# Opening of a Fourier-mixing and GEGLU stack: x loaded one transfer ahead, six rows of tiles in float32, and five S1 tiles summed by transfers

## The chip, the core and the metric

The kernel runs on one core of one Trainium2 chip. The metric is the device time of one execution in microseconds (us); the time before is 1612.5 us, the median of three runs (1612.4 to 1614.12). The engines named below are TensorE (PE, with its weight loads PEld), VectorE (DVE), ScalarE (ACT), GpSimd (POOL) and SyncE (SP). A transfer (DMA) is issued from the instruction stream of SP or of POOL, and an engine executes its own stream in order.

## The reference

```python
def _A_ref(x, dft_seq_re, dft_seq_im, dft_hid_re, dft_hid_im):
    a = jnp.einsum("bsd,ed->bse", x, dft_hid_re)
    b = jnp.einsum("bsd,ed->bse", x, dft_hid_im)
    return jnp.einsum("ts,bse->bte", dft_seq_re, a) - jnp.einsum("ts,bse->bte", dft_seq_im, b)

def _B_ref(x, w_gate, w_up, w_down):
    return (_gelu(x @ w_gate) * (x @ w_up)) @ w_down

x = A_x                                   # (1, 2048, 512) float32
x = x + _A_ref(_layernorm(x), ...)        # layer 0
x = x + _B_ref(_layernorm(x), ...)        # layer 1, hidden size 1792
x = x + _A_ref(_layernorm(x), ...)        # layer 2
x = x + _B_ref(_layernorm(x), ...)        # layer 3
```

## The kernel before

**Arithmetic.** A float32 operand is split into a high part (`hi`, ScalarE, line 147) and a remainder (`lo`, VectorE, line 149), both of type fp32r, and a product of two split operands is three matmuls (`mm3`, lines 196 to 198). The sequence transform of layer 0 and layer 2 is done in four blocks of 512 output rows (`b` = 0 to 3). Real and imaginary parts and the two halves of the sequence make a two by two block product, which is done with seven products in the manner of Strassen and Winograd. Their names are A11, A12, S2, S1, S3, S4 and A22 on the side of the transform (`ws`, 128x512 tiles from memory) and B11, B21, T2, T1, T3, T4 and B22 on the side of the normed rows. Each product runs over `k` = 0 to 7, that is over eight tiles of 128 rows. S1 is A21 + A22, S2 is S1 - A11, S3 is A11 - A21 and S4 is A12 - S2.

**Order of layer 0.** `plan` puts A11 of all four blocks first, then A12 of all four, and then, block by block, S2 (with S1 and S3 two and four steps behind, `skewed(3)`), products with the hidden transform, and S4. For A11 of block 0 alone (`bare`, line 409) nothing is split: `a11` (line 755) multiplies the normed tile `za[k]` and the loaded tile in plain float32 (line 761). Every other product goes through `six` (line 738), which takes two times three matmuls for each `k`. The sums of A12 with A11 for blocks 1 to 3 are added on VectorE (line 184) and put away to memory by POOL (`put_away`, line 251, tensors `m` and `m_sum`). The tiles that they leave are used again as slots.

**Slots and streams.** All 128x512 tiles live in 94 slots (`Slots`, line 98). `items` is the list of what TensorE will take, in order, with the tiles each needs and how it is made; `load_next` (line 285) issues the loads of an item from SP, four items ahead of the splitting, and `split_next` makes it. `make_s2` (line 349) does three VectorE operations on 128x512 tiles: `plus(a22, a21, a22)` (line 187) gives S1, and two `minus` (line 180) give S3 and S2; the split of S2 follows. A load into a slot waits for the last reader of what was in it, and each of the two streams of transfers has eight semaphores in turn, so that a transfer also waits for the one eight places before it.

**The opening.** A row tile of x is loaded (`x_load`, line 224) and normed (`norm_terms`, line 499): VectorE takes the statistics (lines 507 and 509), POOL raises to the power -0.5 (line 515), VectorE makes the shift (line 519), and from the fifth tile on POOL does what VectorE did after line 509 (lines 512 and 517). ScalarE then writes the normed tile (lines 548 and 550), and `first_parts` splits half of it (256 columns, lines 147 and 149). The loads alternate: x 0, ws 0, x 1, ws 1 and so on to x 7 and ws 7 (line 1357). Twelve matmuls on a constant tile (line 1347) come first on TensorE. Steps of the queue `queue` (`opening`, `second_opening`, `combine`, `combine_late`) are run between the products, and put the rest of the norming and the sums T1 to T4 into the streams. The scheduler orders the instructions of each engine from this program when the kernel is built.

**The last layers.** In layer 3 the down products of the first half of the rows are taken from pieces stored in memory (`wc`), and the weights of the second half's first gate and up products (`wb`) are fetched in that stage: `ahead` (line 1282) is a list of eight `piece_load` steps, put at the head of the queue one third of the way through (line 1316), ahead of the steps that bring in and divide the rows of the second half.

Of the kernel before, what the change touches and what calls it, by code (L numbers as in the profile page):

```python
# [14 lines left out]
P = 128  # L15
# [28 lines left out]
def fnet_geglu(ctx: ExitStack, tc: tile.TileContext, x_in, ws, wh, wgu, wdn, wdc, out):  # L44
# [113 lines left out]
    def split_slot(src):  # L158
        hi, lo = sb.get(F32R), sb.get(F32R)
        split(src, hi, lo)  # L160
        return hi, lo
# [20 lines left out]
    def plus(out, a, b):  # L182
        if id(b) in ps8.held:
            bank_read["DVE"] = nc.vector.tensor_tensor(out, a, b, op=ALU.add)  # L184
        else:
            with behind("DVE"):
                nc.vector.tensor_tensor(out, a, b, op=ALU.add)  # L187
# [97 lines left out]
    def load_next():  # L285
        n = stream["loaded"]
        dtype, addresses, _, _ = items[n]
        raws[n] = []
        for a in addresses:
            t = sb.get(dtype)  # L290
            to = t if dtype == F32 else f32(t)
            if len(a.shape) == 3:
                to = to.rearrange("p (h c) -> p h c", h=2)
            stream["last"] = nc.sync.dma_start(to, a)
            raws[n].append(t)
        stream["loaded"] += 1

    def too_far(n):
# [43 lines left out]
    def make_a11(k):  # L342

        def run(v):
            held[k] = v
            return split_slot(v)
        return run

    def make_s2(k):
        def run(a21, a22, *a11):  # L350
            a11 = a11[0] if a11 else held.pop(k)
            plus(a22, a21, a22)
            minus(a21, a11, a21)
            minus(a11, a22, a11)
            s1s[k], s2s[k], s3s[k] = a22, a11, a21
            return split_slot(a11)
        return run

    def make_s1(k):
# [46 lines left out]
            steps += products  # L406
        return steps

    def bare(layer, b, what):

        return layer == 0 and b == 0 and what == "A11"


    NP = NF // 2
# [15 lines left out]
    def mix_items(layer):  # L430
        def raw(make, *tiles):
            items.append((F32, tiles, make, None))

        for b, what in plan(layer):
            tiles = [[ws[(b * 2 + m) * NS + k] for k in range(NS)] for m in range(2)]
            (a11, a12), (a21, a22) = ((r[:NK], r[NK:]) for r in tiles)
            hold = b >= FORE[layer]
            if what == "A11":
                for k in range(NK):
                    raw(as_is if bare(layer, b, what) else make_a11(k) if hold else plain, a11[k])  # L440
            elif what == "A12":
                for k in range(NK):
                    raw(plain, a12[k])
            elif what == "S2":
                for i, k in skewed(3):
                    if i == 0:
                        raw(make_s2(k), a21[k], a22[k], *(() if hold else (a11[k],)))
                    else:
                        raw(make_s1(k) if i == 1 else make_s3(k))
            elif what == "S4":  # L450
                for i, k in skewed(2):
                    if i == 0:
                        raw(make_s4(k), a12[k])
                    else:
                        raw(plain, a22[k])
            else:
                for m, c in what:
                    if layer == 0 and b == 0:
                        items.append((F32, (wh[m * ND + c],), make_hid_first(m, c), (m, c)))
                    else:  # L460
                        items.append((F32R, halves(whs[m, c]), make_hid(m, c), (m, c)))
# [26 lines left out]
            slow.pop(0)()  # L488


    known, shifts = {}, []

    def row_of(layer, i, mixed):
        x = fresh.pop(("mixed", i) if mixed else i, None)
# [4 lines left out]
    def norm_terms(layer, i, x, junk):  # L499

        pool = spool if layer == 0 else kpool
        rstd = pool.tile([P, 1], F32, name="rstd")
        shift = pool.tile([P, 1], F32, name="shift")
        if layer == 0 or layer == 2 and i >= NS - NK:
            st = spool.tile([P, 6], F32, name="st")
            with tc.issue_after(shifts[-1].ins) if layer == 0 and i == 1 else ExitStack():
                nc.vector.bn_stats(st, x)
            mv = spool.tile([P, 2], F32, name="mv")
            nc.vector.bn_aggr(mv, st)
            late = layer == 0 and i >= 4  # L510
            if late:
                nc.gpsimd.tensor_scalar(rstd, mv[:, 1:2], 1.0, EPS, op0=ALU.mult, op1=ALU.add)  # L512
            else:
                nc.vector.tensor_scalar_add(rstd, mv[:, 1:2], EPS)
            nc.gpsimd.tensor_tensor(rstd, rstd, power, op=ALU.pow)
            if late:
                nc.gpsimd.tensor_scalar(shift, mv[:, 0:1], -1.0, rstd, op0=ALU.mult, op1=ALU.mult)
            else:
                shifts.append(nc.vector.scalar_tensor_tensor(shift, mv[:, 0:1], -1.0, rstd, op0=ALU.mult, op1=ALU.mult))  # L519
        else:  # L520

            total = spool.tile([P, 1], F32, name="total")
            mean = spool.tile([P, 1], F32, name="mean")
            nc.scalar.activation(junk, x, AF.Copy, accum_out=total)  # L524
            nc.scalar.activation(mean, total, AF.Copy, scale=-1.0 / D)
            nc.scalar.activation(junk, x, AF.Square, bias=mean, accum_out=rstd)  # L526
            nc.gpsimd.tensor_scalar(rstd, rstd, 1.0 / D, EPS, op0=ALU.mult, op1=ALU.add)  # L527
            nc.gpsimd.tensor_tensor(rstd, rstd, power, op=ALU.pow)
            nc.scalar.activation(shift, mean, AF.Copy, scale=rstd)
        return rstd, shift  # L530
# [30 lines left out]
    def first_parts(k):  # L561
        zparts["11", k] = split_side(za[k][:, half[0]])
# [134 lines left out]
    def mix(layer):  # L697
# [57 lines left out]
        def a11(b):  # L755
            chain = [ps8.get() for _ in range(2)]
            for k in range(NK):
                if bare(layer, b, "A11"):
                    t, = take()
                    for c in range(2):  # L760
                        nc.tensor.matmul(chain[c], za[k][:, c * P:(c + 1) * P], t, start=k == 0, stop=k == NK - 1)
                    sb.put(t)
                    step()
                else:
                    six(chain, "B11", k, k == 0, k == NK - 1, "11" if b == NB - 1 else None)
            sums[b] = [copied(p) for p in chain]
            if b < FORE[layer]:
                ps8.put(*chain)
            else:
                chains[b] = chain  # L770
# [178 lines left out]
    def geglu(w, layer):  # L949
# [333 lines left out]
        if plain_down:  # L1283
            for f in range(NF - LAG, NF):
                down(f, 0)
            add_rows(0)
            if before_mix:
                for k in range(NT):
                    queue.extend([lambda k=k: second_rows(layer + 1, k), lambda k=k: combine(k)])
                queue.extend([lambda k=k: combine_late(k) for k in range(NT)])  # L1290
            else:
                queue.extend(ahead)
            for f in range(NF):
                if f == NF - 2:
                    load_rows(1)
                down(f, 1)
                while len(queue) > 2 * (NF - 1 - f):
                    step()
            add_rows(1, before_mix)
        else:  # L1300
            if pairs == NP:
                pair_combined(NP - 1)
            late = down_order(layer, w)[1]
            for i, (name, k) in enumerate(late):
                for more in late[i:i + EARLY + 1]:
                    prepared(*more)
                for _ in down_product(name, k):
                    pass
                if not before_mix or i % 3 == 0:
                    step()  # L1310
                if before_mix and i == len(late) // 2:
                    stream["more"] = MORE
                if i == len(late) // 3:
                    load_turned(1)
                    if w == 0:
                        queue[:0] = ahead
                while w == 0 and len(queue) > 2 * (len(late) - 1 - i):
                    step()
            if pairs < NP:
                plain_rows()  # L1320
# [31 lines left out]
    def x_ahead(i):  # L1352
        if i < NS and i not in loaded:
            loaded.add(i)
            fresh[i] = x_load(0, i)

    for i in range(NK):
        x_ahead(i)
        load_next()

    def opening(k):

        def run():
            x_ahead(k + 2)
            if k < NK:
                first_norm(0, k)
            first_parts(k - 2)
        return run

    def second_opening(k):  # L1370
# [64 lines left out]
```

## Time and profile before

| what | us |
|---|---|
| median of three runs | 1612.5 |
| the profiled execution, its own time | 1614.3 |
| the profiled execution, span from first to last instruction | 1612.5 |
| PE busy | 1604.7 |
| DVE busy | 1171.6 |
| ACT busy | 816.9 |
| POOL busy | 275.2 |

The profile gives busy times by engine, the idle time ahead of groups of instructions with what ended it, the chain of work that ended last, and a timeline. Starts are counted from the start of the span. A matmul is shown with a busy time longer than the distance to the next one, since matmuls are pipelined; the distance between their starts is what counts. A float32 matmul that is not split shows as two records.

### The profile page before, as it was taken

The page shows a single profiled execution, that of the slowest core. Times are in us where ns is not written, and L with a number is a line of the kernel's source. Part 1 is how long each engine was busy: PE and PEld are TensorE (multiplying, and loading weights), DVE is VectorE, ACT ScalarE, POOL GpSimd, SP SyncE. Part 2 cuts the span into 40 slices and gives each one's busy share as a digit, 9 for nine tenths or more (in the row PEclk, how much of TensorE's full clock was granted, in tenths as well). Part 3 has the DMA queues.
Part 4 walks back from the last instruction along what each step waited for, and adds up shares of the span by engine and source line. Part 5 has one row for each costly group of instructions (what it writes and reads, how often), then busy time and mean ns, then how long its engine had stood idle before and what let it go on. Part 6 is the DMA issues. An engine that isn't in the chain of part 4 may idle for free.

```text
span 1612.5 us, 22750 instructions
## 1 busy us (share of the span) xinstructions
PE 1604.7 (100%) x7046; PEld 1322.2 (82%) x7046; DVE 1171.6 (73%) x2023; ACT 816.9 (51%) x1564; POOL 275.2 (17%) x497
## 2 busy tenths in 40 slices
PE   9999999999999999999999999999999999999999
PEld 6888888888888888888888888888888888888887
DVE  7997878789876665666889978877874557844574
ACT  7753453545766434555757433644445535433360
POOL 3211010142544113220031000110410000000001
PEclk9999999999999999999999999999999999999999
DMA  9767787899978799986895776968989777796455
GB/s 360 240 233 261 263 273 240 267 320 318 349 275 301 226 353 305 378 298 230 290 304 177 251 250 205 315 206 310 273 284 277 236 227 218 242 301 193 147 180 157
DMA packets 250090, 424.67 MB, mean 263 GB/s; under 512 B 28848, under 2 KB 90032, under 8 KB 248944
## 3 DMA queue, kind: packets, MB, share of 16 engines
q1 hardware_dynamic: 223488, 334.33, 65.2%
q0 software_dynamic: 26480, 88.89, 15.0%
q8 instruction: 56, 0.92, 0.2%
q14 instruction: 66, 0.54, 0.1%
HBM read 339.48 MB, written 83.62 MB: 262 GB/s over the span
## 4 chain that ended last, share of the span: by engine, by line
PE 91%; DMA 4%; DVE 2%; issue 1%; POOL 1%; ACT 0%; SPq 0%; DVEq 0%; ACTq 0%; POOLq 0%
PE p L196 30%; PE p L198 30%; PE p L197 30%; DMA s<-ws 2%; DVE s L149 1%; DVE s L180 1%; DMA s<-x 0%; DMA s<-wc 0%; POOL rstd L512 0%; ACT s L147 0%; DMA s<-wb 0%; DMA xwide<-ws 0%; DMA m_sum<-s 0%; DVE s L184 0%; DMA xwide<-t 0%
## 5 line engine op out<-in xcount | busy, mean ns | idle before, releaser
L197 PE MATMUL p<-s,s 128*128 128x512 f32 x2330 | 904.6, 389 | 0.0
L198 PE MATMUL p<-s,s 128*128 128x512 f32 x2330 | 896.1, 389 | 0.0
L196 PE MATMUL p<-s,s 128*128 128x512 f32 x2330 | 864.9, 390 | 1.3 <-DMA s<-wb 0.7
L147 ACT ACTIVATE s<-s 128x512 fp32r<-128x512 f32 (+1 forms) x785 | 445.1, 606 | 327.7 <-PE p L197 66.0
L149 DVE TENSOR_TENSOR s<-s,s 128x512 fp32r<-128x512 f32 (+1 forms) x785 | 492.1, 660 | 92.7 <-ACT s L147 76.9
L196 PEld LDWEIGHTS p<-s,s 128*128 128x128 f32 x2330 | 437.1, 188 | 94.3 <-ACT s L147 2.2
L197 PEld LDWEIGHTS p<-s,s 128*128 128x128 f32 x2330 | 437.3, 188 | 91.2 <-DVE s L149 0.3
L198 PEld LDWEIGHTS p<-s,s 128*128 128x128 f32 x2330 | 437.3, 188 | 90.8
L184 DVE TENSOR_TENSOR s<-s,p 128x512 f32<-128x512 f32 x286 | 192.5, 682 | 211.7 <-PE p L198 120.3
L191 ACT ACTIVATE s<-p 128x512 f32<-128x512 f32 x218 | 127.6, 592 | 133.1 <-PE p L198 121.3
L180 DVE TENSOR_TENSOR s<-s,s 128x512 f32<-128x512 f32 (+1 forms) x323 | 192.5, 612 | 2.0 <-DMA s<-ws 0.7
L946 ACT ACTIVATE s<-s 128x512 f32<-128x512 f32 x103 | 64.7, 629 | 87.3 <-DVE s L184 85.5
L147 ACT ACTIVATE s<-xwide 128x512 fp32r<-128x512 f32 x83 | 50.8, 622 | 65.7 <-PE p L197 14.0
L527 POOL TENSOR_SCALAR rstd<-rstd 128x1 f32<-128x1 f32 x40 | 20.7, 518 | 341.4 <-ACT s L526 335.0
L149 DVE TENSOR_TENSOR s<-xwide,s 128x512 fp32r<-128x512 f32 x83 | 56.0, 681 | 23.6 <-ACT s L147 23.2
L278 POOL DMA_DIRECT2D wb<-s x84 | 45.4, 543 | 58.3 <-ACT s L147 45.8
L550 ACT ACTIVATE s<-s,shift,rstd 128x512 f32<-128x512 f32 x56 | 45.0, 810 | 19.7 <-DVE shift L519 9.4
L524 ACT ACTIVATE s<-s 128x512 f32<-128x512 f32 x33 | 20.8, 630 | 64.2 <-PE p L198 34.1
L960 DVE TENSOR_TENSOR s<-s,s 128x512 f32<-128x512 f32 x75 | 51.7, 689 | 1.8
L240 POOL DMA_DIRECT2D x<-s x31 | 17.0, 549 | 141.1 <-DVE s L184 134.4
L187 DVE TENSOR_TENSOR s<-s,s 128x512 f32<-128x512 f32 (+1 forms) x67 | 39.5, 607 | 0.6 <-DMA s<-wgu 0.6
L184 DVE TENSOR_TENSOR xwide<-s,p 128x512 f32<-128x512 f32 x13 | 8.9, 687 | 41.5 <-PE p L198 41.5
(97 smaller groups left out, 567.8 us busy)
## 6 DMA issues: line engine op xcount, KB each, us to landing
s<-ws SPq DMA_DIRECT2D x384, 256.0 KB, 4.5
s<-wb SPq DMA_DIRECT2D x294, 256.0 KB, 5.1
s<-wc SPq DMA_DIRECT2D x133, 256.0 KB, 4.4
s<-wh SPq DMA_DIRECT2D x116, 256.0 KB, 5.1
wb<-s POOLq DMA_DIRECT2D x98, 256.0 KB, 4.4
s<-x SPq DMA_DIRECT2D x63, 256.0 KB, 5.4
xwide<-ws SPq DMA_DIRECT2D x52, 256.0 KB, 5.0
wc<-s POOLq DMA_DIRECT2D x49, 256.0 KB, 6.0
```

The source lines that it names most:

```text
L147: newest["ACT"] = nc.scalar.activation(hi, src, AF.Copy)
L149: newest["DVE"] = nc.vector.tensor_tensor(lo, src, f32(hi), op=ALU.subtract)
L180: nc.vector.tensor_tensor(out, a, b, op=ALU.subtract)
L184: bank_read["DVE"] = nc.vector.tensor_tensor(out, a, b, op=ALU.add)
L191: bank_read["ACT"] = nc.scalar.activation(v, src, AF.Copy)
L196: nc.tensor.matmul(ps, ah, bh, start=start, stop=False, skip_group_check=True)
L197: nc.tensor.matmul(ps, ah, bl, start=False, stop=False, skip_group_check=True)
L198: nc.tensor.matmul(ps, al, bh, start=False, stop=stop, skip_group_check=True)
L278: nc.gpsimd.dma_start(a, f32(t))
L550: nc.scalar.activation(z, x, AF.Identity, bias=shift, scale=rstd)
L946: nc.scalar.activation(t, g, AF.Gelu_apprx_tanh)
L960: nc.vector.tensor_tensor(t, t, v, op=ALU.mult)
```

## The change

Five edits are made together.

- The first loads are x 0, then x 1, ws 0, x 2, ws 1 and so on: x is one transfer ahead of ws, and x 8 is loaded ahead of ws 7.
- A11 of block 0 is done in plain float32 for `k` = 0 to 5 alone. For `k` = 6 and 7 it goes through `six`, in the same accumulation, so that two more ws tiles are split, and the splits of the normed tiles 6 and 7 are made earlier (`opening`).
- On VectorE the statistics of a row tile of layer 0 are issued after the small operations of the tiles one and two before it.
- For block 0 of layer 0 and `k` = 3 to 7, S1 is not added on VectorE. After the load of an item, POOL issues a transfer that reads A21 from memory a second time and adds it to the A22 tile on chip.
- In layer 3 the eight `piece_load` steps are put into the queue in turn with the steps already there, and no longer all ahead of them.

```diff
@@ load_next
             stream["last"] = nc.sync.dma_start(to, a)
             raws[n].append(t)
+        if getattr(items[n][2], "summed", False):
+            nc.gpsimd.dma_start(raws[n][1], addresses[0], accum_op=ALU.add)
@@ make_s2
-    def make_s2(k):
+    def make_s2(k, summed):
         def run(a21, a22, *a11):
             a11 = a11[0] if a11 else held.pop(k)
-            plus(a22, a21, a22)
+            if not summed:
+                plus(a22, a21, a22)
             minus(a21, a11, a21)
             minus(a11, a22, a11)
...
+        run.summed = summed
@@ bare, mix_items
-    def bare(layer, b, what):
-        return layer == 0 and b == 0 and what == "A11"
+    def bare(layer, b, what, k):
+        return layer == 0 and b == 0 and what == "A11" and k < 6
...
-                        raw(make_s2(k), a21[k], a22[k], *(() if hold else (a11[k],)))
+                        raw(make_s2(k, layer == 0 and b == 0 and k >= 3), a21[k], a22[k], *(() if hold else (a11[k],)))
@@ norm_terms
-            with tc.issue_after(shifts[-1].ins) if layer == 0 and i == 1 else ExitStack():
+            late = layer == 0 and i >= 4
+            with ExitStack() as order:
+                if layer == 0:
+                    for at in (("rstd", i - 1), ("shift", i - 2)):
+                        if at in first_small:
+                            order.enter_context(tc.issue_after(first_small[at].ins))
                 nc.vector.bn_stats(st, x)
@@ a11
-                        nc.tensor.matmul(chain[c], za[k][:, c * P:(c + 1) * P], t, start=k == 0, stop=k == NK - 1)
+                        nc.tensor.matmul(chain[c], za[k][:, c * P:(c + 1) * P], t, start=k == 0, stop=False, skip_group_check=True)
@@ geglu
-                        queue[:0] = ahead
+                        queue[:2 * len(ahead)] = [run for pair in zip(ahead, queue) for run in pair] + queue[len(ahead):2 * len(ahead)]
@@ the opening
+    x_ahead(0)
     for i in range(NK):
-        x_ahead(i)
+        x_ahead(i + 1)
         load_next()
...
-            first_parts(k - 2)
+            for j in (k - 2,) if k < 7 else (5, 6) if k == 7 else (k - 1,) if k <= NK else ():
+                first_parts(j)
```

More of the change, by code (lines that the diff above doesn't have):

```diff
@@ L439, in mix_items @@
                 for k in range(NK):
-                    raw(as_is if bare(layer, b, what) else make_a11(k) if hold else plain, a11[k])
+                    raw(as_is if bare(layer, b, what, k) else make_a11(k) if hold else plain, a11[k])
             elif what == "A12":
@@ L488, in step @@
             slow.pop(0)()
-    known, shifts = {}, []
+    known, first_small = {}, {}
     def row_of(layer, i, mixed):
@@ L509, in norm_terms @@
             nc.vector.bn_aggr(mv, st)
-            late = layer == 0 and i >= 4
             if late:
@@ L513, in norm_terms @@
             else:
-                nc.vector.tensor_scalar_add(rstd, mv[:, 1:2], EPS)
+                first_small["rstd", i] = nc.vector.tensor_scalar_add(rstd, mv[:, 1:2], EPS)
             nc.gpsimd.tensor_tensor(rstd, rstd, power, op=ALU.pow)
@@ L518, in norm_terms @@
             else:
-                shifts.append(nc.vector.scalar_tensor_tensor(shift, mv[:, 0:1], -1.0, rstd, op0=ALU.mult, op1=ALU.mult))
+                first_small["shift", i] = nc.vector.scalar_tensor_tensor(
+                    shift, mv[:, 0:1], -1.0, rstd, op0=ALU.mult, op1=ALU.mult
+                )
         else:
@@ L757, in a11 @@
             for k in range(NK):
-                if bare(layer, b, "A11"):
+                if bare(layer, b, "A11", k):
                     t, = take()
                     for c in range(2):
-                        nc.tensor.matmul(chain[c], za[k][:, c * P:(c + 1) * P], t, start=k == 0, stop=k == NK - 1)
+                        nc.tensor.matmul(chain[c], za[k][:, c * P:(c + 1) * P], t, start=k == 0, stop=False, skip_group_check=True)
                     sb.put(t)
```

## The prediction

> **What bounds the kernel now.** I read the page first: busy times, clock, groups. Columns of a group: line, engine, operation, tiles and count | busy us, mean ns | idle ahead of it and what ended it.
>
> ```profile
> PE 1604.7 (100%) x7046; PEld 1322.2 (82%) x7046; DVE 1171.6 (73%) x2023; ACT 816.9 (51%) x1564; POOL 275.2 (17%) x497
> PEclk9999999999999999999999999999999999999999
> ...
> L196 PE MATMUL p<-s,s 128*128 128x512 f32 x2330 | 864.9, 390 | 1.3 <-DMA s<-wb 0.7
> ```
>
> PE is busy for 1604.7 of 1612.5 at an even clock, and the first of each three matmuls waits only 1.3 us in all. So only two things can gain: less work for PE, and the few places where PE stands. The view of PE's waits (total, times, longest) names these.
>
> ```profile
> PE p L761 <- ACT s L550: 1.5, 1, 1.5
> PE p L1347 <- POOL ident masks.py:199: 1.4, 1, 1.4
> PE p L196 <- DMA s<-wb: 0.7, 1, 0.7
> PE p L196 <- ACT s L147: 0.5, 1, 0.5
> ```
>
> Some 4 us, of which 1.4 lies ahead of the constant tile and isn't touched. The other three are places that the change touches. Of shared limits, the windows (PE, PEld, DVE, ACT, POOL busy of 20, clock, DMA share, GB/s) show one:
>
> ```profile
> 60.00:80.00 20.00, 20.00 (x90) 16.55 (x89) 20.00 (x43) 14.14 (x26) 0.60 (x2) 1.00 0.64 207
> 80.00:100.00 20.00, 19.90 (x88) 16.14 (x86) 20.00 (x34) 8.53 (x15) 2.16 (x4) 1.00 0.88 302
> 100.00:120.00 20.00, 19.56 (x86) 16.05 (x87) 20.00 (x34) 12.84 (x23) 2.70 (x5) 1.00 0.47 151
> ```
>
> From 60 to 120 us DVE has no gap. There, a PE that arrives earlier finds DVE where it was.
>
> **The change part by part.** The sums are made against the profiled execution's own time, 1614.3; the median, 1612.5, is 1.8 below it, and I take the same difference off at the end.
>
> *A, two tiles less in plain float32.* A plain pass loads its weights every 0.43 us, a split one steps every 0.23:
>
> ```profile
> 12.26 0.19 PEld L761 LDWEIGHTS p<-s,s 128*128 128x128 f32 x1 [0.24 <-issue]
> ...
> 13.98 0.19 PEld L761 LDWEIGHTS p<-s,s 128*128 128x128 f32 x1 [0.24 <-issue]
> ...
> 25.16 0.39 PE L196 MATMUL p<-s,s 128*128 128x512 f32 x1
> ...
> 26.52 0.39 PE L196 MATMUL p<-s,s 128*128 128x512 f32 x1
> ```
>
> The first two rows are four passes apart, one k of two column halves: 1.72. The last two are six split matmuls apart: 1.36. Two k save 2 x 0.36 = **0.72**, certain unless the splits come late. They add two splits of 512 columns on ACT and two on DVE.
>
> *B, x one transfer ahead.*
>
> ```profile
> 6.20 1.88 PE L761 MATMUL p<-s,s 128*128 128x512 f32 x4
> 6.21 0.69 DVE L507 BATCH_NORM_STATS2 st<-s 128x6 f32<-128x512 f32 x1 [0.85 <-DMA s<-x]
> ...
> 7.59 0.69 DVE L507 BATCH_NORM_STATS2 st<-s 128x6 f32<-128x512 f32 x1 [0.28 <-DMA s<-x]
> ...
> 8.52 0.15 DVE L519 SCALAR_TENSOR_TENSOR shift<-mv,rstd 128x1 f32<-128x1 f32 x1
> ...
> 9.58 7.99 PE L761 MATMUL p<-s,s 128*128 128x512 f32 x18 [1.50 <-ACT s L550]
> ```
>
> x 1 is third in line and its statistics start at 6.21; x 2, fifth, at 7.59. As second in line x 1 is about two places sooner, near 4.1 (the third and fifth are 1.38 apart, 0.69 a place, and the first row is at the time of the third). Its shift, however, stands on DVE behind the statistics of x 2, which is now fourth and lands near 6.9: 6.9 + 0.69 = 7.6 in place of 8.52. The normed tile then reaches PE at 9.58 - 0.9 to 1.0 = 8.6. The first product ends at 6.20 + 1.72 = 7.92, so 0.65 of 1.66 remains: **-1.0**. The bounds: -1.4, if the shift slips in ahead of those statistics, and -0.4, if ws 0, third now and needed at 6.20, is late too.
>
> *C, the tighter rows after it.* Behind it PE asks for a normed tile each 1.72, 1.0 sooner than before and at the end every 1.36, while ACT gives one per 1.9:
>
> ```profile
> 14.25 0.81 ACT L550 ACTIVATE s<-s,shift,rstd 128x512 f32<-128x512 f32 x1
> ...
> 16.14 0.81 ACT L550 ACTIVATE s<-s,shift,rstd 128x512 f32<-128x512 f32 x1 [0.62 <-POOL shift L517]
> ```
>
> Part of A and B can be lost here: 0 to +1.0. The tiles are some 2 us ahead of their use, so I take the lower end, **+0.3**.
>
> *D, five sums made by transfers.* DVE loses five operations of 0.60 (from 112.25 to 112.86 below) and gains two splits: -1.8. Of this, only one sum, k = 3, lies ahead of the place where PE stands, against two splits: +0.6 there. That place is the stage change:
>
> ```profile
> 94.20 0.68 DVE L184 TENSOR_TENSOR s<-s,p 128x512 f32<-128x512 f32 x1
> ...
> 95.17 0.54 POOL L251 DMA_DIRECT2D m_sum<-s  x1 [1.26 <-DVE s L184]
> ...
> 99.76 3.24 ACT L147 ACTIVATE s<-s 128x512 fp32r<-128x512 f32 x6 [2.41 <-DMA m_sum<-s]
> ...
> 100.44 1.25 PE L196 MATMUL p<-s,s 128*128 128x512 f32 x4 [0.54 <-ACT s L147]
> ...
> 103.60 1.14 POOL L251 DMA_DIRECT2D m_sum<-s  x2 [7.88 <-DVE s L184]
> ...
> 112.25 0.68 DVE L187 TENSOR_TENSOR s<-s,s 128x512 f32<-128x512 f32 x1
> 112.86 0.68 DVE L149 TENSOR_TENSOR s<-s,s 128x512 fp32r<-128x512 f32 x1
> ```
>
> DVE's last addition at 94.20 releases POOL's put-away at 95.17, whose landing lets ACT use that slot for a split at 99.76, for which PE waits: 0.88 in all with the two short gaps behind it (PE's next matmuls stand 0.1 further apart than 0.23). In the built order POOL issues two accumulations, for k = 3 and 4, between the first pair of these put-aways and the second, and each waits for its tile to land; k = 5 and 6 stand ahead of the third pair, and k = 7 behind it. Each costs POOL an issue of 0.54. Two extra issues (1.08) and two DVE operations (0.6 net) push the release later, and A and B bring PE there 1.4 sooner; against them, DVE stood still for 2.47 earlier and might not:
>
> ```profile
> 45.94 5.63 POOL L512 TENSOR_SCALAR rstd<-mv 128x1 f32<-128x1 f32 x1 [2.25 <-DVE mv L509]
> ...
> 53.99 0.42 DVE L180 TENSOR_TENSOR s<-s 128x256 f32<-128x256 f32 x1 [2.47 <-ACT s L550]
> ```
>
> Bounds: -0.88 (DVE is 2.47 ahead, and the wait vanishes) and +2.2 (1.4 sooner + 0.6 + 0.2 of issues that aren't covered). Between them I take **+0.7**, half of the 1.4 given back. The accumulation itself isn't in the trace; its nearest rows are transfers of the same size, counted here with the median from issue to landing:
>
> ```profile
> s<-ws SPq DMA_DIRECT2D x24, 256.0 KB, 4.3
> m_sum<-s POOLq DMA_DIRECT2D x6, 256.0 KB, 4.4
> ```
>
> I take 4.4 to 9 (a read of each operand as a transfer of its own); up to 9 it is covered, as worked out under the third rival. The 1.3 MB more are 5 x 0.68 (a transfer's step in E below), laid over a stretch whose share of DMA was 0.88 and then 0.47: no PE time, unless the loads ahead of them slip.
>
> *E, pieces in turn in layer 3.*
>
> ```profile
> 1372.55 0.32 SPq L936 DMA_DIRECT2D s<-wb  x1
> 1373.23 0.37 SPq L294 DMA_DIRECT2D s<-wc  x1
> ```
>
> The chain of waits at that place (start, us, what):
>
> ```profile
> 1370.52 5.37 DMA s<-wb
> 1375.89 0.04 issue
> 1375.94 0.50 PE p L196
> ```
>
> PE waits here for a piece issued at 1370.52. SP's stream goes out one transfer per 0.68 there; in the built order the piece needed first stands one place earlier, 0.68 of the 0.83 that PE loses (0.7 in the view of waits, the rest in the two starts after it): **-0.6**, bounds -0.83 and 0 (the queue is full and another piece is waited for).
>
> *Sum*: -0.72 - 1.0 + 0.3 + 0.7 - 0.6 = -1.3; 1614.3 - 1.3 = 1613.0, which is **1611.2** as a median. 0.2% is 3.2 us, about what a measurement of this kernel can tell from no change; the forecast lies inside it.
>
> **The rivals.**
> *First: everything is kept.* The stall of 2.47 on DVE isn't repeated, and the stage change gives -0.65 in place of +0.7: 1611.2 - 1.35 = **1609.8**, and 1608.7 with every term at its better bound (-0.72 - 1.4 - 0.88 - 0.83 = -3.8). For it: 45.94 is the one long run of L512, by chance of order. Against it: 20.00 of 20 on DVE after it.
> *Second: the change doesn't do what it says.* DVE and the put-aways fix the release at 100.44, PE arrives earlier and waits longer, and A to C are gone: only E and noise remain, 1614.3 - 0.6 + 0.3 = 1614.0, **1612.2**.
> *Third, the slower side: accumulations that are slow.* The last one, for k = 7, adds to a tile loaded into the slot that the last put-away frees (issued from 103.60, and ACT gets such a slot at 108.06 below); the tile is in near 110 (an estimate: 108.06 and some 2 us on a queue at 0.47). Before, S1 was ready at 112.25 + 0.68 = 112.93, and ACT had 4.21 to spare a little later:
>
> ```profile
> 108.06 1.67 ACT L147 ACTIVATE s<-s 128x512 fp32r<-128x512 f32 x3 [1.63 <-DMA m_sum<-s]
> ...
> 123.20 0.63 ACT L147 ACTIVATE s<-s 128x512 fp32r<-128x512 f32 x1 [4.21 <-DVE s L180]
> ```
>
> ACT's stream is in order, so all later splits queue behind this one. At 9 us it lands at 119, 6.1 later, 4.2 absorbed: +1.9, still about no change (D's +0.7 is then replaced: 1612.4). From 12 us on it decides; at 13.5, three plain transfers, it lands at 123.5, 10.6 late, 6.4 on PE: 1611.2 + 6.4 - 0.7 = **1616.9**. Against it: nothing in the trace moves 256 KB as slowly on an open queue.
> *Fourth: DVE starves the transfers that POOL issues.* If accumulations issued near 91 only moved when DVE pauses, at its first long gap, which ends at 127.70, the splits of block 0 would be 127.7 - 112.9 = 14.8 late; less ACT's 4.2, that is 10.6 on PE in place of the forecast's 0.7: 1611.2 + 9.9 = **1621**.
>
> ```profile
> 127.70 0.69 DVE L149 TENSOR_TENSOR s<-s,s 128x512 fp32r<-128x512 f32 x1 [3.14 <-ACT s L147]
> ```
>
>  The put-aways speak against it: one is issued by POOL at 95.17 with DVE at 20.00 of 20, and ACT takes its slot at 99.76, 4.6 later. The Trainium skill, page "SBUF — State Buffer", section "SBUF: two separate sides", states such a trap: while a VectorE operation holds the port pair shared with GpSimd, GpSimd can't write the descriptors of the transfers that it issues. By that rule this change would move work onto the worst of queues; the trace agrees for a compute operation of POOL (5.63 at 45.94 while DVE ran without a break) and not for its transfers.
>
> **How the numbers follow.** Forecast 0.36 (own range 1609.8 to 1612.5), first rival 0.34, second 0.10, third 0.16, fourth 0.04. Faster by over 0.2% means below 1609.3: the better part of the first rival, 0.20. Slower, above 1615.7: third and fourth, 0.20. The rest, 0.60, is no change. The range leaves out the fourth and the outer part of the third: 1608.8 to 1616.4.
>
> **What would show it.** A: two k fewer on L761 and PE's busy time 0.7 lower. B: the wait of L761 for L550 at 0.6 to 0.7, not 1.5. C: new waits for L550 or L147 between 10 and 20 us. D: the wait for L147 near 99 at about 1.2 to 1.6, and the rows of the new transfers at 4.4 to 9 us. E: no wait for wb near 1375. I'm wrong if the accumulations take over 12 us, if PE has a wait above 2 us between 100 and 130, or if the start of layer 2 moves by other than -1.5 to +1.

## The result and the profile after

The change is slower: 1616.72 us, the median of 13 runs (1614.21 to 1619.22), against 1613.92 for the kernel before in 13 runs of its own (1612.40 to 1616.73). The ratio is 1.0018, with a 95% interval of 1.0011 to 1.0025. The profiled execution of after has a span of 1616.4 and a time of its own of 1618.2, that is 1.5 above its median; that of before is 0.4 above the median of its 13 runs. Single traces are therefore compared place by place here, and medians decide on the whole.

The page of after, in the same rows as before, and then the view of TensorE's waits (total, times, longest):

```profile
PE 1607.3 (99%) x7050; PEld 1325.5 (82%) x7050; DVE 1170.6 (72%) x2020; ACT 820.7 (51%) x1566; POOL 270.7 (17%) x502
...
L196 PE MATMUL p<-s,s 128*128 128x512 f32 x2334 | 870.8, 390 | 3.8 <-ACT s L147 3.1
```

```profile
PE p L196 <- ACT s L147: 3.1, 1, 3.1
PE p L1357 <- POOL ident masks.py:199: 1.4, 1, 1.4
PE p L196 <- DMA s<-wb: 0.6, 1, 0.6
PE p L197 <- DVE s L149: 0.4, 1, 0.4
```

The wait of 1.5 us in the opening is gone. The wait at the stage change has grown from 0.5 to 3.1, and the one for `wb` in layer 3 is what it was. PE's busy time rose by 2.6 us, although the change takes work from PE. Why it did shows in the timeline of PE behind the wait, and in the windows there (PE, PEld, DVE, ACT, POOL busy, clock, DMA share, GB/s):

```profile
103.00 1.65 PE L196 MATMUL p<-s,s 128*128 128x512 f32 x3 [3.12 <-ACT s L147]
104.45 0.63 PE L197 MATMUL p<-s,s 128*128 128x512 f32 x1
104.87 0.63 PE L198 MATMUL p<-s,s 128*128 128x512 f32 x1
...
109.37 0.39 PE L197 MATMUL p<-s,s 128*128 128x512 f32 x1
109.60 0.39 PE L198 MATMUL p<-s,s 128*128 128x512 f32 x1
```

```profile
101.00:105.00 4.00, 2.00 (x5) 1.61 (x6) 2.02 (x4) 2.68 (x6) 0.66 (x2) 0.66 0.67 183
105.00:109.00 4.00, 4.00 (x11) 3.13 (x10) 4.00 (x7) 1.65 (x4) 1.35 (x3) 0.50 0.95 240
```

After the wait the matmuls stand 0.43 apart instead of 0.23 for some 6 us, at a granted clock of 0.50. Added up over these starts, the excess over 0.227 is 3.0 us, behind a gap of 3.3. So this place costs 6.3 us, where it cost 0.9 before. The page of after shows nines for the clock in all 40 slices: a slice is 40 us long, and 6 us of half clock don't show in it. Narrow windows show where the clock falls:

```profile
102.20:102.30 0.10, 0.00 (x0) 0.00 (x0) 0.00 (x0) 0.00 (x0) 0.00 (x0) 1.00 1.07 246
102.30:102.40 0.10, 0.00 (x0) 0.00 (x0) 0.00 (x0) 0.08 (x1) 0.00 (x0) 0.50 1.16 246
```

It falls at 102.30, while TensorE still stands (its last matmul ends at 99.88), and is back at 109.13, 6.83 us later.

Where the wait comes from is read in POOL's stream, in the last rows of VectorE ahead of it, and in the chain of waits. Here line 297 is a transfer that sums, and line 251 a put-away. First POOL:

```profile
91.22 0.92 POOL L297 DMA_DIRECT2D s<-ws  x1 [10.36 <-ACT s L147]
93.48 0.88 POOL L297 DMA_DIRECT2D s<-ws  x1 [1.35 <-DMA s<-ws]
94.05 1.44 POOL L251 DMA_DIRECT2D m_sum<-s  x2
97.77 0.89 POOL L297 DMA_DIRECT2D s<-ws  x1 [2.27 <-DMA s<-ws]
104.34 0.88 POOL L297 DMA_DIRECT2D s<-ws  x1 [5.68 <-DMA s<-ws]
104.90 1.45 POOL L251 DMA_DIRECT2D m_sum<-s  x2
```

VectorE:

```profile
88.37 0.68 DVE L184 TENSOR_TENSOR s<-s,p 128x512 f32<-128x512 f32 x1
...
90.77 0.68 DVE L184 TENSOR_TENSOR s<-s,p 128x512 f32<-128x512 f32 x1
```

And the chain (start, us, what):

```profile
87.15 5.75 DMA s<-ws
92.90 0.02 issue
92.93 0.04 POOLq L297
...
94.05 0.46 POOL m_sum L251
94.51 0.11 issue
94.62 7.68 DMA m_sum<-s
102.30 0.02 issue
102.32 0.64 ACT s L147
```

VectorE finishes the second sum of block 2 at 90.77 + 0.68 = 91.45, 3.4 us earlier than before (94.20 + 0.68). Its put-away could go at once, but POOL stands at the transfer that sums k = 4, and that one waits until the tile it adds to has landed (the load in the chain, done at 92.90). So the put-away (the second of the pair in the row at 94.05) is issued at 94.62, 3.2 us after its data were ready. Then it takes 7.68 us to land, against 4.56 before, behind the two transfers that sum. Their kind has the longest median of the stretch from 80 to 110 us, by the view of transfers (count, KB each, median us to landing):

```profile
s<-ws SPq DMA_DIRECT2D x19, 256.0 KB, 5.4
m_sum<-s POOLq DMA_DIRECT2D x6, 256.0 KB, 5.6
s<-ws POOLq DMA_DIRECT2D x4, 256.0 KB, 6.4
```

The slot comes free at 102.30 instead of 99.74, and PE, which is 1.6 us ahead of before by then, stands. Counted from the last matmul, the one that waits here comes seven places behind the one that waited before, 7 x 0.227 = 1.6 us of work; so the wait is 2.4 us longer, and not the 4.2 (2.56 + 1.6) that the two differences add up to.

### The profile page after: what moved, and what is told of

The parts are those of the page before. It is cut to its first block, busy times and chain, and to the rows that moved or that the text cites. A ratio compares the mean times of both kernels' runs of the same rounds, so it can differ in the third digit from the quotient of the medians.

```text
span 1616.4 us, 22760 instructions
## 1 busy us (share of the span) xinstructions
PE 1607.3 (99%) x7050; PEld 1325.5 (82%) x7050; DVE 1170.6 (72%) x2020; ACT 820.7 (51%) x1566; POOL 270.7 (17%) x502
## 4 chain that ended last, share of the span: by engine, by line
PE 96%; DMA 2%; DVE 1%; issue 0%; ACT 0%; POOL 0%; POOLq 0%; SPq 0%; DVEq 0%; ACTq 0%
PE p L197 32%; PE p L196 32%; PE p L198 32%; DVE s L149 1%; PE p L771 1%; DMA s<-x 1%; DMA m_sum<-s 0%; DMA s<-ws 0%; DMA s<-wb 0%; PE p L1357 0%; ACT s L147 0%; DVE s L184 0%; DVE s L180 0%; DVE s L1202 0%; ACT s L560 0%
## 5 line engine op out<-in xcount | busy, mean ns | idle before, releaser
L537 POOL TENSOR_SCALAR rstd<-rstd 128x1 f32<-128x1 f32 x40 | 13.2, 331 | 351.8 <-ACT s L536 346.2
```

## The experiments

The table sums up all kernels. "Offset" is the start of one and the same matmul in the profiled execution less its start in that of before (counted from the last matmul, so that added or removed ones at the front don't matter); negative is earlier. "Ratio" is that of the times against before, with its interval.

| kernel | median us | ratio | offset at 30 us | at 115 us | at the end |
|---|---|---|---|---|---|
| the change | 1616.72 | 1.0018 [1.0011, 1.0025] | -1.6 | +3.7 | +3.9 |
| e1 sums on VectorE | 1612.37 | 0.9996 [0.9987, 1.0005] | -1.8 | -2.7 | -2.6 |
| e2 summing transfers alone | 1617.68 | 1.0027 [1.0017, 1.0037] | -0.5 | +5.8 | +5.5 |
| e3 put-aways first | 1613.41 | 0.9997 [0.9988, 1.0006] | -0.9 | -1.8 | -1.1 |
| e4 ten more matmuls | 1616.23 | 1.0016 [1.0007, 1.0025] | -1.3 (the ten added matmuls, 2.27, taken off) | +1.6 | +2.0 |
| e5 opening alone | 1612.58 | 0.9991 [0.9982, 1.0000] | -1.7 | -2.6 | -1.7 |
| e6 pieces in turn alone | 1613.89 | 0.9999 [0.9990, 1.0008] | -0.6 | -1.5 | -2.1 |
| e7 six rows alone | 1613.45 (one run) | none | -0.9 | -1.9 | -0.8 |
| e8 x ahead alone | 1613.99 (one run) | none | -0.7 | -0.2 | -0.3 |
| e9 small operations on VectorE | 1615.17 | 1.0007 [0.9997, 1.0016] | 0.0 | +0.1 | +0.7 |
| e10 opening and small operations | 1613.31 | 0.9998 [0.9989, 1.0007] | -1.9 | -2.8 | -1.3 |

**e1: the sums on VectorE again.**

```diff
-make_s2(k, layer == 0 and b == 0 and k >= 3)
+make_s2(k, False)
```

> The change without its transfers that sum: S1 of all tiles is added on VectorE again. Theory 1 (the put-aways of the second pair stand on POOL behind two of these transfers, so that a slot comes free late): the wait of 3.1 us of TensorE for ScalarE at 103 us and the half clock behind it are gone, PE's start offset against before stays at -1.6 to -2.5 us from there on, and the time is 0.998 to 0.999 of before. Rival (the earlier opening alone brings TensorE too early to the stage change): a wait of 2 to 3 us is still there and the time is at least 1.001 of before.

TensorE's waits:

```profile
PE p L1357 <- POOL ident masks.py:199: 1.4, 1, 1.4
PE p L196 <- DMA s<-wb: 1.2, 1, 1.2
```

POOL's stream:

```profile
89.13 0.54 POOL L251 DMA_DIRECT2D m_sum<-s  x1 [8.49 <-DVE s L184]
91.53 0.54 POOL L251 DMA_DIRECT2D m_sum<-s  x1 [1.86 <-DVE s L184]
```

The wait at the stage change is gone, and the put-away goes out at 91.53, as soon as its sum is there. The early opening isn't what causes the wait, so the rival falls. By the ratios the kernel is some 3.5 us better than the change (0.9996 against 1.0018, and the intervals don't meet), but at most 1 us better than before and not clear of it: the expected 0.998 to 0.999 was missed.

**e2: the summing transfers alone,** in the kernel before.

```diff
             raws[n].append(t)
+        if getattr(items[n][2], "summed", False):
+            nc.gpsimd.dma_start(raws[n][1], addresses[0], accum_op=ALU.add)
...
-            plus(a22, a21, a22)
+            if not summed:
+                plus(a22, a21, a22)
```

> The kernel before with the five summing transfers alone. Theory 1: the put-away that TensorE waits for at 100 us lands near 102 instead of 99.7, so the wait grows from 0.7 to about 2.5 to 3 us: 2 us slower, or 5 us with half the clock behind it (1.001 to 1.003). Rival (it needs the opening as well): within 0.5 us of before.

The chain of waits at the stage change, and PE's clock behind it:

```profile
89.28 5.41 DMA s<-ws
...
95.26 0.52 POOL s L297
...
96.38 7.19 DMA m_sum<-s
```

```profile
105.00:109.00 4.00, 4.00 (x11) 3.17 (x10) 4.00 (x7) 2.46 (x5) 1.15 (x2) 0.50 0.75 201
```

The same chain as in the change, without its opening: a load, a summing transfer that waited for it, a put-away of over 7 us, a wait of 3.1 and half the clock. Of the five edits this one alone makes the loss. The ratio is larger here (1.0027), as it would be without the opening's gain beside it, but its interval overlaps that of the change.

**e3: the same transfers, the put-aways first.** Only the order on POOL is changed, for k = 3 and 4.

```diff
-        nc.gpsimd.dma_start(away[key], t)
+        newest["away"] = nc.gpsimd.dma_start(away[key], t)
...
-            nc.gpsimd.dma_start(raws[n][1], addresses[0], accum_op=ALU.add)
+            with tc.issue_after(newest["away"].ins) if items[n][2].summed < 5 else ExitStack():
+                nc.gpsimd.dma_start(raws[n][1], addresses[0], accum_op=ALU.add)
```

> The change with the summing transfers of k = 3 and 4 placed on POOL behind the second pair of put-aways, nothing else moved. Theory 1 (order on POOL): these put-aways are issued near 91.5 us and land before 99, no wait over 1 us at the stage change, time 0.998 to 0.999 of before. Rival (the summing transfers slow all transfers by their traffic): the put-aways still take over 7 us from issue to landing, or a later tile is waited for, and the time stays at 1.001 or above.

```profile
90.31 0.54 POOL L251 DMA_DIRECT2D m_sum<-s  x1 [8.69 <-DVE s L184]
92.70 0.54 POOL L251 DMA_DIRECT2D m_sum<-s  x1 [1.86 <-DVE s L184]
93.38 0.92 POOL L298 DMA_DIRECT2D s<-ws  x1
94.52 0.88 POOL L298 DMA_DIRECT2D s<-ws  x1 [0.22 <-issue]
```

All five transfers are still there, and no wait is left at the stage change (the waits of PE at 1.0 and above are those for the constant tile and for `wb`). The second pair, issued at 90.31 and 92.70, landed after 5.8 and 5.3 us, not over 7. The traffic does slow the transfers a little (from 80 to 110 us a median of 5.2 for loads and 5.5 for put-aways, against 4.3 and 4.4 before), but nothing waits for it. This settles it: the order on POOL makes the loss, not the traffic. It also shows what the transfers are worth when they hold up nothing. At 0.9997 against e1's 0.9996, five additions less on VectorE bring nothing that can be measured.

**e4: ten matmuls more** of no use, on a spare bank ahead of the wait.

```diff
+            if layer == 0 and b == NB - 1:
+                spare, any_hi = ps8.get(), zparts["T12", 0][0]
+                for _ in range(10):
+                    nc.tensor.matmul(spare, any_hi[:, :P], any_hi, start=True, stop=True)
+                ps8.put(spare)
```

> The change with ten extra 128x512 matmuls of no use (2.27 us at full clock) on TensorE just ahead of the place where it waits at 103 us. Theory 1 with a clock that falls after an idle time near 3 us: the wait is 1 us, the clock stays full, and the kernel is about 3 us faster than the change, though it does more (0.999 to 1.0005 of before). Rival (the half clock belongs to the place, or the late tile moves with the work): the wait and the half clock stay, and the time is that of the change or 2 us above it.

The timeline and the windows of PE:

```profile
102.09 0.97 PE L196 MATMUL p<-s,s 128*128 128x512 f32 x3 [1.26 <-ACT s L147]
102.89 0.39 PE L197 MATMUL p<-s,s 128*128 128x512 f32 x1
103.12 0.40 PE L198 MATMUL p<-s,s 128*128 128x512 f32 x1
```

```profile
101.00:105.00 4.00, 2.91 (x13) 2.42 (x14) 2.93 (x5) 3.24 (x6) 1.59 (x3) 1.00 0.77 174
105.00:109.00 4.00, 4.00 (x19) 3.33 (x18) 4.00 (x8) 1.70 (x3) 0.43 (x1) 1.00 1.01 302
```

With the wait at 1.26 the clock stays at 1.00, so the half clock belongs to the wait and not to the place. In the traces e4 stands 2.2 us ahead of the change at 115 us, for 2.27 us more work. The medians don't show the 3 us that were expected: 1.0016 against 1.0018. The 13 runs of the change offer an explanation, though they don't prove it. Three of them had a mean clock of 1.000 and took 1614.2 to 1614.9, the three at 0.998 took 1617.9 to 1618.2, and the rest, at 0.999, 1615.2 to 1619.2. Half the clock for 6.83 us lowers the mean of 1616 us by 0.002. So the change seems to pay from nothing to some 3 us for the clock in an execution; where the clock stays full, ten more matmuls only cost. The length of the wait need not be all that decides: in all twelve traces, each stretch at one clock that ends before the kernel does lasts a whole multiple of 3.413 us (6.827, 95.573, 98.987, 1508.691, 1604.264 or 1607.677), so that the clock seems to be set in steps of that length, and where a wait falls in them may count too. No run tests it, and what the clock costs the median stays open.

**e5: the opening alone** (the change without summing transfers, with line 1316 of before).

```diff
-                        queue[:2 * len(ahead)] = [run for pair in zip(ahead, queue) for run in pair] + queue[len(ahead):2 * len(ahead)]
+                        queue[:0] = ahead
```

> The change without the summing transfers and without the pieces in turn in layer 3: only the opening is left. If the pieces in turn are worth what the prediction gave them (0.6 us), the wait for wb near 1373 us is 0.6 us longer than the 1.2 of the kernel without the summing transfers alone, near 1.8, and the time 0.6 us above that kernel's 1612.4. If they are worth nothing, the wait is 1.0 to 1.4 and the time is 1612 to 1612.8, 0.999 to 1.000 of before.

```profile
PE p L196 <- ACT s L147: 1.0, 1, 1.0
PE p L196 <- DMA s<-wb: 0.3, 1, 0.3
```

Without the pieces in turn the wait for `wb` is 0.3, not 1.8 and not even the 1.2 of e1. The wait of 1.0 for ScalarE is at 378 us, where e10 shows 0.7 and before nothing. The ratio of e5, 0.9991, is the lowest of all kernels run, but the interval touches 1, so that even this gain isn't clear of no change.

**e6: the pieces in turn alone,** in the kernel before, the reverse of the diff of e5.

> The kernel before with the pieces in turn alone. Prediction: TensorE's wait for wb of 0.7 us is 0.1 us or gone, 0.6 us faster. Rival (one place earlier in the queue is lost again, since SP's loads wait for slots that TensorE frees): wait 0.5 to 0.8, no difference from before.

```profile
PE p L1347 <- POOL ident masks.py:199: 1.4, 1, 1.4
PE p L198 <- DMA s<-wb: 0.4, 1, 0.4
PE p L761 <- ACT s L550: 0.4, 1, 0.4
```

No difference in time. The wait for `wb` is a little shorter here than in before (0.4 against 0.7), but over all profiles the edit shows nothing: 0.4, 0.6, 0.7, 1.2 and 1.2 with it, 0.2, 0.3, 0.5, 0.5, 0.6 and 0.7 without, and none in e2. Two other waits of this trace are more telling. Its opening is that of before, and yet the wait of L761 is 0.4 instead of 1.5; and it has no wait at 100 us at all.

**e7 and e8: six rows alone, and x ahead alone** (with its order of the statistics), one run each.

```diff
-        return layer == 0 and b == 0 and what == "A11"
+        return layer == 0 and b == 0 and what == "A11" and k < 6
```

> The kernel before with six rows of tiles in float32 alone. Prediction: TensorE stands 0.72 us ahead of before from 30 us on. Rival (the splits come late): new waits of TensorE between 15 and 21 us take 0.4 us or more of it. By 100 us the wait for the put-away is longer by what was won, so that the end moves by less than 0.3 us.

```diff
+    x_ahead(0)
     for i in range(NK):
-        x_ahead(i)
+        x_ahead(i + 1)
         load_next()
```

> The kernel before with x one transfer ahead and its order of the statistics alone. Prediction: the wait for the second normed tile falls from 1.5 to about 0.6 us, and TensorE stands 1.0 us ahead of before from 30 us on. The change's own trace has no such wait at all, so 1.5 ahead is the other value. If DVE's stall of 2.47 us at 54 us is there, the wait at 100 us takes most of it; if it is gone, the gain reaches the end.

e7 stands 0.9 ahead at 30 us, but its own wait in the opening is 0.8 shorter than that of before by the execution, and its first product starts 0.44 later (6.64 against 6.20, as in e6 and in the change). Beside e6, which has the opening of before and starts at 6.64 too, it is 0.36 ahead with a wait 0.32 longer (0.69 against 0.37): 0.68 for the two tiles, where the forecast was 0.72. In e8 no wait for the second normed tile is left in the view of waits, and TensorE stands 0.7 ahead, not 1.0. At 100 us e7 has no wait, and e8 has 1.3 (1.1 in the view of waits). The difference lies at 54 us, in VectorE's idle time; the rows of e8 on POOL and VectorE:

```profile
48.28 4.01 POOL L516 TENSOR_SCALAR rstd<-mv 128x1 f32<-128x1 f32 x1
...
54.19 0.43 DVE L180 TENSOR_TENSOR s<-s 128x256 f32<-128x256 f32 x1 [1.95 <-ACT s L556]
```

Only the profiles of before and e8 have a long operation of this kind on POOL (5.63 and 4.01 us; up to e7 elsewhere at most 1.3), only they have an idle time of VectorE near 54 us (2.47 and 1.95), and of all kernels without summing transfers only they have a wait at 100 us. e6, the same program as before up to layer 3, has none of the three. So that wait of before looks like an accident of the execution, not a part of the kernel.

**e9 and e10: those small operations on VectorE,** in before and in e5.

```diff
-            late = layer == 0 and i >= 4
+            late = layer == 0 and 4 <= i < 8
```

> The kernel before with the small operations on the statistics of the second eight row tiles on VectorE instead of POOL (nothing else of the change). Theory: TensorE's wait at 100 us in the profile of before came from one operation of POOL that took 5.63 us beside VectorE's run without a break; without that operation on POOL, VectorE has no idle time over 1 us between 40 and 60 us, no wait is left at 100 us, and the median is 0 to 1 us below before, since only some executions have the long operation. Rival: VectorE's own small operations wait for POOL's power in its stream and cost more than they save, 1 us or more slower, with idle times of VectorE between 20 and 50 us.

> The opening alone (no summing transfers, no pieces in turn) with the same small operations on VectorE. Theory: as the opening alone, which had no long operation of POOL in its profile, so 1612 to 1612.8 and 0.999 of before, at most 0.5 us better than the opening alone. Rival: VectorE waits for POOL in its stream, and the time is that of before or above it.

Both were misses. The wait at 100 us is gone in e9, as expected, but 1.0 us of new gaps stand at 93 to 94 us, and the median is 1.3 us above before. In e10 VectorE waits for POOL twice (0.44 and 0.46 us), and the opening's gain shrinks to nothing that can be measured. Neither is clear of before, by its interval. The edit also didn't take the long operation away. POOL still raises to the power, and in both profiles that operation is now the long one, 2.75 us at 46.09 in e10 and in e9:

```profile
47.40 3.35 POOL L515 TENSOR_TENSOR rstd<-rstd,power 128x1 f32<-128x1 f32 x1 [1.97 <-DVE rstd L514]
```

VectorE's waits of 0.46, in e9 at 50.79 and in e10 at 48.87, end with it.

## Why the prediction was wrong

**The step that failed is D**, in the sentence "Each costs POOL an issue of 0.54". The prediction had the right place, the right order on POOL and even "each waits for its tile to land", and then priced only the two issues (1.08). The issue itself was of that size: the put-away starts 0.57 behind the second one (93.48 to 94.05). What they cost is the wait of the instruction at the head of POOL's stream: the put-away was held 3.2 us (91.45 to 94.62), and behind the transfers ahead of it, it landed in 7.68 instead of 4.56 us. In e1, with nothing ahead of it, the same put-away was issued at 91.53 and landed in 5.0; so of 5.8 us that the slot came free later, 3.1 are the hold and 2.7 the slower landing. The term was +0.7 with an upper bound of +2.2. Measured in the traces, the place went from 0.9 to 6.3, that is +5.4: 2.4 of that is longer waiting, already outside the bounds, and 3.0 is the clock. The half clock was in neither the sum nor the bounds; no wait of before, 1.5 us at the longest, shows one. One of the prediction's own signs of being wrong came true, a wait above 2 us between 100 and 130.

The Trainium skill, page "TensorE: Matmul & The Clock Gate", section "Part 1: The HAM clock gate", says that TensorE's clock falls to half after at least one idle window of about 3.4 us. The runs agree in that gaps of 3.3 and 3.4 us between matmuls brought a clock of 0.50, and one of 1.4 did not. But so long a time without work was not needed: the clock fell 2.4 us after the end of the last matmul in the change (99.88 to 102.30), and in e2 2.1 us after it (101.17 to 103.26, with a gap of 0.8 just ahead).

**A to C, the opening**, forecast -0.72 - 1.0 + 0.3 = -1.4 by 30 us: -1.6 in the change, -1.7 and -1.8 in e5 and e1. That the sum agrees is in part luck, by two errors that nearly cancel. B left 0.65 of the wait of 1.5, and none stayed. Against that, the first product of the change starts 0.44 later than that of before (6.64 against 6.20), and not by the edits, for e6 does so too. It follows the clock, which is full from 5.7 us on in before and from 6.7 and 6.9 in the change and e6: up to there the matmuls on the constant tile stand 0.21 apart, behind it 0.11. Beside e6 the change is 1.0 us ahead at 30 us, and not 1.6. The medians of e5 and e1 gain as much, 1.1 and 1.0 us, though neither is clear of no change. The wait that B removes is long in some executions (1.6 in e9, 1.5 in before) and short in others (0.4 in e6, 0.7 in e7); B was sized by one execution in which it is long.

**E, the pieces in turn**, forecast -0.6: nothing (e6, 0.9999). One place earlier in SP's stream didn't bring the piece one step of 0.68 earlier, as e1 and the change show: the wait for `wb` stayed or grew. Why the place was lost again wasn't tested.

**The rivals.** The first one's condition held: VectorE's stall of 2.47 wasn't there in the change or in most runs, and without the summing transfers "everything is kept" is what the traces of e1 and e5 show up to 115 us (-2.7 and -2.6). By the medians it is worth 1.0 and 1.1 us, not the 2.7 of its 1609.8. The second fell with the same two kernels: TensorE arrives earlier there and finds no wait at the stage change. The third looked at the right edit and took the wrong transfers: not the last one for k = 7, by its own duration of 12 us, but the two for k = 3 and 4, by standing ahead of the put-aways. The summing transfers took a median of 6.4 us to land in the change, inside the 4.4 to 9 of the forecast. The fourth fell with that number: transfers that were starved until VectorE's long gap would have taken over 30 us.

## What to carry to other kernels

A transfer that waited for its data held what stood behind it on the engine that issues it, here a ready put-away for 3.2 us. So price a new one by how long it can stand at the head of that stream, by who waits for the next one in it, and by how much later that one lands, not by its issue. A relief for a busy engine is worth only what the engine's lateness costs: here VectorE was busy for 20.00 of 20 us around the place, and five operations less brought nothing that could be measured. Where a change makes one wait of TensorE longer, look at the clock behind it, in windows of a few microseconds; and take a wait as part of a kernel only if more than one execution shows it.

## What the runs showed of the hardware

- The row of a transfer that adds to a tile on chip lasts 0.88 to 0.92 us on POOL in the change, that of a plain put-away 0.54, and 0.88 right behind a summing one; yet the next one starts 0.57 behind (93.48, 94.05, 94.62). The summing ones landed after a median of 6.4 us, beside 5.6 for put-aways and 5.4 for loads in the same stretch of the change.
- TensorE's clock was at half for 6.83 us from 102.30 (the change) and from 103.26 (e2), with gaps of 3.3 and 3.4 us between its matmuls there, which cost 3.0 us more in the change; the fall came 2.4 and 2.1 us after the end of the last matmul.
- In all twelve traces the stretches at one clock that end before the kernel does are whole multiples of 3.413 us.
- One operation of POOL on 128x1 elements took 5.63 us (before), 4.01 (e8), 3.35 (e9) and 2.75 (e10), starting at 46 to 48 us beside a run of VectorE without a break; in the other eight profiles none took over 1.1 us in that stretch.
